# Attention heads kept stacked by partition, with their inverse row sums spread through DRAM, in an adaLN transformer block

## The chip, the cores and the metric

The kernel runs on one core of one Trainium2 chip. The metric is the device time of one execution in microseconds (us); less is better. The core's engines are TensorE (PE; its weight loads are PEld), VectorE (DVE), ScalarE (ACT), GpSimd (POOL) and SyncE (SP), which here issues nearly all DMAs, in program order, and waits in that order too.

## The reference

One transformer block on a sequence of 2048 rows with model width 448: layer norm with a modulation from a condition vector, windowed attention with 16 heads of width 28 (each row sees itself and the 255 rows before it), output projection, residual; then layer norm and modulation again and an MLP of width 1792 with the Mish function, and a residual.

```python
def _A_ref(x, wqkv, wo):          # H = 16, Dh = 28, W = 256
    q, k, v = qkv[0], qkv[1], qkv[2]
    scores = jnp.einsum("bhqd,bhkd->bhqk", q, k) * (Dh ** -0.5)
    mask = (idx[:, None] - idx[None, :] >= 0) & (idx[:, None] - idx[None, :] < W)
    p = _softmax(jnp.where(mask[None, None], scores, -1e9), axis=-1)
    o = jnp.einsum("bhqk,bhkd->bhqd", p, v)
    return o.transpose(0, 2, 1, 3).reshape(B, S, D) @ wo

h = _layernorm(x) * (1 + ca) + sa
x = x + ga * _A_ref(h, A_wqkv, A_wo)
h = _layernorm(x) * (1 + cb) + sb
x = x + gb * _B_ref(h, B_w1, B_b1, B_w2)     # dense, Mish, dense
```

## The kernel before

All large products are done in two halves: a number is split into a high part that the fast matmul type holds and a low remainder, and a product is high x high + high x low + low x high. So each operand has a "hi" copy (ScalarE) and a "lo" subtraction (VectorE or GpSimd).

The 2048 rows are four groups of 512. Group 0's norm and its first q and k tiles come first. q and k go to DRAM (`scr`) split and come back per head with `L`. Then runs the attention loop over u = 0 to 191, three steps per head, 48 steps per group. In each step TensorE does: the low and high half products with v of two older steps (`PV`, into a bank named pv), the scores of this step with their mask (`B`, bank sB), one or two score tiles whose row maxima VectorE takes (`A`, bank sA, two buffers), and some filler. ScalarE takes the exponential of sB twice (P and its high part Ph), GpSimd subtracts (`SP`: Pl = P - Ph), and Pl is multiplied two steps later. Every second head a transpose of the row maxima (`M2`, tile mt) and two small DMAs (q<-mr) put them back into q.

Filler is the other matmul work: q, k and v of the next group, the output projection of the group before, turns of the norm's output. Generators yield after each chunk with its estimated cost, and a credit of 0.56 to 0.87 per step (`RATE`) decides how many chunks a step takes. A filler that has nothing to do yields too and uses up the credit. Group 3 has no next group, so its filler ends near its step 28.

The part that is changed: after a head's last PV, `EV` (L751) copies 60 rows of pv (28 of V's high part, the row sums at row 28, from row 32 the 28 of V's low part) into one half of `o2`. For every pair of heads `E` (L759) turns that tile with four transposes into bank et, `E2` (L764, ScalarE) copies the low part, `E3` takes the reciprocal of the sums (L772, VectorE), adds the low part (L773, VectorE) and multiplies (L775, GpSimd) into `on`, where rows are sequence positions. When a group is full, `gen_oT` (TensorE L250, ScalarE L624, VectorE L619) turns it back, 16 transposes a group, into oh and ol, and `gen_wo` multiplies four 128-row tiles with wo, 11 matmuls each.

After the loop come nine more steps with the last PVs and the first MLP tiles (`TAIL`), then the MLP: for each group 14 f tiles, each 11 matmuls into z (`f1_mm`), Mish on ScalarE, and 12 into four acc banks (`ff2`). During the first group w1 and w2 are still being loaded and split (`pieces`, `piece_load`), group 3's projection runs as filler (`fill`), and the second group's norm as `fill2`. Ahead of this MLP loop SyncE issues `x1_load(0)`, pieces 4 to 8 of a list, and `x1_load(1)`.

Of the kernel before, what the change touches and what calls it, by code (L numbers as in the profile page):

```python
# [51 lines left out]
def adaln_block(ctx: ExitStack, tc: tile.TileContext, x, wqkv, wo, w1, b1, w2, c, w_mod, out):  # L52
# [36 lines left out]
    x1d = dram.tile([S, D], F32, name="x1d")  # L89
    xnd = dram.tile([NG - 1, GT, 512], F32, name="xnd")  # L90
# [221 lines left out]
    def tile_mms(p, ps):  # L312
        m = 0
        for n, (a, b) in enumerate(ps):
            PE.matmul(p, b, a, start=(n == 0), stop=(n == 10))  # L315
            m += 1
            if m >= chunk["v"] and n < 10:
                yield cost(m, p.shape[-1])
                m = 0
        return cost(m, p.shape[-1])  # L320
# [180 lines left out]
    first_tiles([(0, bank("pv", 1, "qk0_0")), (3, bank("tr", 1, "qk0_3"))])  # L501
# [17 lines left out]
    O2 = []  # L519
    for i in range(2):  # L520
        t = att.tile([128, GT], F32, name=f"o2_{i}")
        POOL.memset(t[32:64, :], 0.0)
        O2.append(t)
    wo3 = [mid.tile([128, D], F32R, name=f"wo3_{i}", tag="wo", bufs=7) for i in range(4)]
    wol = [mid.tile([128, D], F32R, name=f"wol_{i}", tag="wo", bufs=7) for i in range(3)]
# [25 lines left out]

    def gen_mod_wo():
# [7 lines left out]
        for ci in range(4):  # L560
            t = stg(qk, f"wop{ci}")
            pieces.append(t[:, 0:D])
            later.append(lambda ci=ci, t=t: load_piece(wo, ci, 0, D, t))
            yield
        yield
        flush()
        for ci in range(4):
# [5 lines left out]
            split_lo(w, wo3[ci], wol[min(ci, 2)], ci, DVE)  # L573
# [33 lines left out]
    on = {}  # L607
# [3 lines left out]
    on_full = set()  # L611
    XR = {g: {} for g in range(NG)}

    def gen_oT(g, tag, bufs, oT_pool, own=""):
        o = on[g]
        oh, ol = OT[g] = new_T(f"o{g}", oT_pool, own)

        def oT_out(p, ci):
            DVE.tensor_tensor(ol[:, ci], p, oh[:, ci].bitcast(F32), op=ALU.subtract)  # L619

        for ci in range(4):
            p = bank(tag, bufs, f"ot{g}{ci}")
            tr_chunk([o[:, t] for t in range(4)], ci, p)
            ACT.activation(oh[:, ci], p, AF.Copy)  # L624
            pipe.add(1, lambda p=p, ci=ci: oT_out(p, ci))
            if ci < 3:
                later.append(lambda t=ci: xr_load(g, t))
            yield
            if g == NG - 1:
                yield  # L630
# [6 lines left out]
    def gen_wo(g, tag, bufs, beside=None):  # L637
# [14 lines left out]
        for t in range(4):  # L652
# [12 lines left out]
            yield w  # L665
            if beside is not None and t:
                yield next(beside)
# [5 lines left out]
    mx, Pt, Ph, Pl, pvb, et, olt = {}, {}, {}, {}, {}, {}, {}  # L673
# [15 lines left out]
    def M2(pr):  # L689
        p = bank("tr", 1, f"mt{pr}")  # L690
# [56 lines left out]

    def EV(i):
        o = O2[i // 2 % 2][64 * (i % 2):64 * (i % 2) + 60]
        if i < NS - 3:  # L750
            ACT.activation(o, pvb[i][0:60, :], AF.Copy)  # L751
        else:
            DVE.tensor_copy(o, pvb[i][0:60, :])

    def E(pr):
        g, h = divmod(2 * pr, H)
        p = bank("tr", 1, f"et{pr}")
        for t in range(4):
            PE.transpose(p[:, t * 128:t * 128 + 124], O2[pr % 2][0:124, t * 128:(t + 1) * 128], ident[0:124, 0:124])  # L759
        et[pr] = p.rearrange("p (t a d) -> p t a d", t=4, a=2)  # L760

    def E2(pr):
        olt[pr] = att.tile([128, 4, 2, 28], F32, name=f"ol{pr}", tag="ol", bufs=1)
        ACT.activation(olt[pr], et[pr][:, :, :, 32:60], AF.Copy)  # L764

    def E3(pr):
        g, h = divmod(2 * pr, H)
        e, ol = et[pr], olt[pr]
        if h == 0:
            on[g] = mid.tile([128, 4, 512], F32, name=f"on{g}", tag="on")  # L770
        rc = att.tile([128, 4, 2, 1], F32, name=f"rc{pr}", tag="rc", bufs=2)
        DVE.reciprocal(rc, e[:, :, :, 28:29])  # L772
        DVE.tensor_tensor(ol, ol, e[:, :, :, 0:28], op=ALU.add)  # L773
        o = on[g][:, :, h * DH:(h + 2) * DH].rearrange("p t (a d) -> p t a d", a=2)
        POOL.tensor_tensor(o, ol, rc.to_broadcast([128, 4, 2, 28]), op=ALU.mult)  # L775
        if h == H - 2:
            POOL.tensor_copy(on[g][:, :, D:512], on[g][:, :, 384:448])
            on_full.add(g)
# [100 lines left out]
    def w2_split(f):  # L879
        n = NF - 1 - f  # L880
        pl = FW["p1"] if f == 0 else FW["ff"]
        w2h[f] = (mid.tile([128, D], F32R, name=f"w2h{f}", tag="wo", bufs=7) if n < 7 else
# [151 lines left out]
    credit = 0.0  # L1034
    for u in range(NU + 9):
# [21 lines left out]
        if s % 2 == 1 and 1 <= (s - 1) // 2 <= NS // 2:  # L1057
            pr = (s - 3) // 2
            if k == 2 and pr >= 0:
                E(pr)  # L1060
        if s % 2 == 0 and k < 2 and 0 <= (s - 4) // 2 < NS // 2:
            (E2, E3)[k]((s - 4) // 2)
# [81 lines left out]

# [62 lines left out]
```

## Time and profile before

| what | value |
|---|---|
| median of 3 runs | 705.66 us (704.79 to 706.11) |
| span of the profiled execution, first to last instruction | 703.9 us |
| the median less that span | 1.8 us |
| attention loop, first sB matmul to the start of its last step | 48.3 to 405.4 us |
| group starts in it (groups 1, 2, 3) | 122.0, 221.6, 321.8 us |
| MLP, first z matmul to the end | 406.7 to 703.9 us |
| granted TensorE clock | 1.000 |

The span runs from the first to the last instruction. The profiled execution is one execution; its time outside the span is not recorded, so it stands beside the runs by its span.

How to read it: a row of the groups gives line, engine, operation, output and inputs by tile names, shapes and count, then busy time, mean duration in ns, and the idle time before with what ended it. A row of the table of stretches gives the stretch in us from the span's start, its length and each engine's busy time with its number of instructions, then granted clock, DMA share and GB/s. A row of the chain of waits gives start, time on the chain, and what. A matmul's duration is longer than the time until the next one can start.

### The profile page before, as it was taken

The page shows a single profiled execution, that of the slowest core. Times are in us where ns is not written, and L with a number is a line of the kernel's source. Part 1 is how long each engine was busy: PE and PEld are TensorE (multiplying, and loading weights), DVE is VectorE, ACT ScalarE, POOL GpSimd, SP SyncE. Part 2 cuts the span into 40 slices and gives each one's busy share as a digit, 9 for nine tenths or more (in the row PEclk, how much of TensorE's full clock was granted, in tenths as well). Part 3 has the DMA queues.
Part 4 walks back from the last instruction along what each step waited for, and adds up shares of the span by engine and source line. Part 5 has one row for each costly group of instructions (what it writes and reads, how often), then busy time and mean ns, then how long its engine had stood idle before and what let it go on. Part 6 is the DMA issues. An engine that isn't in the chain of part 4 may idle for free.

```text
span 703.9 us, 11999 instructions
## 1 busy us (share of the span) xinstructions
PE 685.9 (97%) x4001; PEld 590.2 (84%) x4001; DVE 383.3 (54%) x1030; ACT 391.6 (56%) x740; POOL 326.4 (46%) x355
## 2 busy tenths in 40 slices
PE   9899999999999999999999899999999999999997
PEld 8777888888888888898887788878888888888886
DVE  5688658788655887655768755452224222421112
ACT  3628788777667867667878974344233323332221
POOL 6626779686666776666778957212010000000000
PEclk9999999999999999999999999999999999999999
DMA  7865664455662462663773165800350035001001
GB/s 209 259 221 188 208 204 152 139 181 157 181 209 76 158 207 88 185 211 95 226 216 120 54 203 170 227 20 1 104 117 4 0 106 119 1 1 52 1 1 52
DMA packets 75178, 90.16 MB, mean 128 GB/s; under 512 B 31535, under 2 KB 51741, under 8 KB 75117
## 3 DMA queue, kind: packets, MB, share of 16 engines
q1 hardware_dynamic: 74652, 89.39, 42.0%
q8 instruction: 32, 0.52, 0.3%
q14 instruction: 30, 0.24, 0.1%
q10 hardware_dynamic: 464, 0.00, 0.0%
HBM read 56.60 MB, written 32.51 MB: 127 GB/s over the span
## 4 chain that ended last, share of the span: by engine, by line
PE 78%; DVE 6%; DMA 6%; ACT 3%; POOL 3%; issue 3%; SPq 1%; DVEq 0%; POOLq 0%; ACTq 0%
PE z L917 17%; PE pv L745 10%; PE qk L315 8%; PE sA L683 5%; PE acc L1106 5%; PE acc L1104 5%; PE acc L1105 5%; PE sB L713 5%; PE wo L315 4%; PE qk_v L315 4%; PE sB L724 3%; DMA scr<-st 2%; PE et L759 2%; PE warm L428 1%; DVE junk L685 1%
## 5 line engine op out<-in xcount | busy, mean ns | idle before, releaser
L735 POOL TENSOR_TENSOR Pl<-P,Ph 128x512 fp32r<-128x512 f32 (+2 forms) x192 | 234.8, 1230 | 80.9 <-ACT Ph L728 46.6
L685 DVE CUSTOM_DVE_ANT_0 junk<-sA,mask 128x384 f32<-128x384 f32 (+2 forms) x256 | 135.1, 528 | 95.1 <-PE sA L683 87.4
L727 ACT ACTIVATE P<-sB 128x512 f32<-128x512 f32 (+2 forms) x192 | 109.6, 571 | 62.3 <-PE sB L724 58.1
L925 DVE TENSOR_TENSOR al<-t,ah 128x512 fp32r<-128x512 f32 x56 | 39.2, 700 | 181.8 <-ACT ah L924 181.8
L923 ACT ACTIVATE t<-z,b1c 128x512 f32<-128x512 f32 x56 | 38.3, 684 | 138.6 <-PE z L917 138.6
L728 ACT ACTIVATE Ph<-sB 128x512 fp32r<-128x512 f32 (+2 forms) x192 | 109.2, 569 | 0.0
L683 PE MATMUL sA<-k,q 84*128 84x384 f32 (+2 forms) x256 | 100.5, 396 | 1.8 <-DVE mx L685 1.1
L917 PE MATMUL z<-hlf,w 128*128 128x512 f32 x224 | 88.6, 395 | 0.0
L917 PE MATMUL z<-hhf,w 128*128 128x512 f32 x224 | 88.6, 395 | 0.0
L1104 PE MATMUL acc<-w2h,ah 128*128 128x448 f32 x224 | 82.2, 367 | 1.2 <-ACT ah L924 1.2
L1106 PE MATMUL acc<-w2h,al 128*128 128x448 f32 x224 | 82.1, 366 | 0.1
L1105 PE MATMUL acc<-w2l,ah 128*128 128x448 f32 x224 | 81.6, 364 | 0.0
L745 PE MATMUL pv<-Ph,v 128*60 128x256 f32 (+2 forms) x352 | 76.7, 292 | 0.6 <-ACT o L751 0.5
L745 PE MATMUL pv<-Pl,v 128*60 128x256 f32 (+2 forms) x352 | 74.0, 284 | 2.4 <-POOL Pl L735 1.4
L713 PE MATMUL sB<-q,k 86*128 86x256 f32 (+1 forms) x352 | 74.2, 285 | 0.5 <-DMA q<-mr 0.5
L917 PE MATMUL z<-hhf,w1l 128*128 128x512 f32 x168 | 66.3, 395 | 0.0
L713 PEld LDWEIGHTS sB<-q,k 86*128 86x128 f32 x352 | 61.5, 189 | 2.3 <-DMA q<-mr 1.5
L724 PE MATMUL sB<-fdmask,identr 128*128 128x128 bf16 (+1 forms) x320 | 60.1, 253 | 0.0
L745 PEld LDWEIGHTS pv<-Ph,v 128*60 128x60 f32 x352 | 45.8, 133 | 14.0 <-ACT o L751 1.9
L745 PEld LDWEIGHTS pv<-Pl,v 128*60 128x60 f32 x352 | 45.2, 132 | 11.5 <-POOL Pl L735 3.8
L683 PEld LDWEIGHTS sA<-k,q 84*128 84x128 f32 x256 | 48.9, 193 | 7.0 <-DVE mx L685 4.3
L917 PEld LDWEIGHTS z<-hlf,w 128*128 128x128 f32 x224 | 42.2, 188 | 10.0
(159 smaller groups left out, 1252.4 us busy)
## 6 DMA issues: line engine op xcount, KB each, us to landing
scr<-st SPq DMA_DIRECT2D x24, 512.0 KB
k<-scr SPq DMA_DIRECT2D x48, 252.0 KB
q<-scr SPq DMA_DIRECT2D x64, 168.0 KB
scr<-st SPq DMA_DIRECT2D x32, 256.0 KB
x<-x1d SPq DMA_DIRECT2D x10, 448.0 KB
xin<-in_A_x_dram SPq DMA_DIRECT2D x8, 448.0 KB
xr<-in_A_x_dram SPq DMA_DIRECT2D x16, 224.0 KB
x1d<-xr SPq DMA_DIRECT2D x16, 224.0 KB
```

Source lines behind the costliest of these rows:

```text
L315: PE.matmul(p, b, a, start=(n == 0), stop=(n == 10))
L683: PE.matmul(p[:, c0:384], q[0:84, t * 128:(t + 1) * 128], k[0:84, t * 128 + c0:t * 128 + 384], start=True, stop=True)
L685: DVE.tensor_tensor_reduce(out=junk[:, c0:384], in0=p[:, c0:384], in1=mask[:, c0:384], scale=1.0, scalar=-3.0e38, op0=ALU.add, op1=ALU.max ...
L713: PE.matmul(p[:, c:c + 128 * (t1 - t0)], k[:, jj * 128:(jj + 1) * 128], q[:, t0 * 128:t1 * 128], start=(n == 0), stop=False, skip_group_ch ...
L727: ACT.activation(P[:, c0:], p[:, c0:], AF.Exp, scale=SCALE)
L728: ACT.activation(Ph[u][:, c0:], p[:, c0:], AF.Exp, scale=SCALE)
L735: eng.tensor_tensor(Pl[u][:, a:b], Pt[u][:, a:b], Ph[u][:, a:b].bitcast(F32), op=ALU.subtract)
L745: PE.matmul(pv[0:60, t0 * 128:t1 * 128], V[j % NV][:, h, :], P[u][:, c:c + 128 * (t1 - t0)], start=(P is Ph and b == 0 and n == 0), stop=F ...
L917: PE.matmul(zb[n], ps[m][1], ps[m][0], start=(m == 0), stop=(m == 10))
L1104: PE.matmul(p, ah[n][:, ts], w2h[f], start=(f == 0), stop=False)
L1105: PE.matmul(p, ah[n][:, ts], w2l[f], start=False, stop=False)
L1106: PE.matmul(p, al[n][:, ts], w2h[f], start=False, stop=(f == NF - 1))
```

## The change

Head outputs are no longer turned. `EV` puts each head into 32 partitions of `on[:, ci]` (four heads a tile, 16 heads in four tiles): ScalarE copies rows 0 to 31 of pv, and VectorE adds the low part's 28 rows in place. The row sums then stand in one partition per head. For each quad of heads, four DMAs spread the sums over 32 partitions of 16 numbers (`sums`), VectorE takes 128x16 reciprocals (`inverse`), one DMA stores them to DRAM (`spread`, tensor rcd), four DMAs read each head's 512 numbers back into 32 partitions (`gather`, tile r4), and GpSimd multiplies the whole tile (`divide`). Counted from step 14 + 12n of the loop, these come at steps 4, 5, 7 and 9 for quad n; `sums` comes one step after each `EV`. Then `split_o` makes hi and lo from `on` at once, without transposes. The tile's 32 rows a head hold 28 numbers, so wo is loaded to 32 rows a head with zeros between, and each wo tile has 12 matmuls, not 11. The last quad's gather is issued after the loop and its divide stands in `gen_split`, in the MLP's first steps. mt moves to the sA banks and pv has two banks.

```diff
-    first_tiles([(0, bank("pv", 1, "qk0_0")), (3, bank("tr", 1, "qk0_3"))])
+    first_tiles([(0, bank("pv", 2, "qk0_0")), (3, bank("pv", 2, "qk0_3"))])
...
+    def wo_rows(ci, t):
+        for j in range(4):
+            r = (4 * ci + j) * DH
+            dma(t[32 * j:32 * j + DH], wo[r:r + DH, :])
...
-            t = stg(qk, f"wop{ci}")
-            pieces.append(t[:, 0:D])
-            later.append(lambda ci=ci, t=t: load_piece(wo, ci, 0, D, t))
+            t = stg(qk, f"wop{ci}")[:, 0:D]
+            pieces.append(t)
+            POOL.memset(t, 0.0)
+            later.append(lambda ci=ci, t=t: wo_rows(ci, t))
...
-    def gen_oT(g, tag, bufs, oT_pool, own=""):
...
+    def split_o(g, ci, pl, own):
+        if ci == 0:
+            OT[g] = new_T(f"o{g}", pl, own)
+        oh, ol = OT[g]
+        ACT.activation(oh[:, ci], on[:, ci], AF.Copy)
+
+        def low():
+            DVE.tensor_tensor(ol[:, ci], on[:, ci], oh[:, ci].bitcast(F32), op=ALU.subtract)
+            if ci == 3:
+                on_split.add(g)
...
+        pipe.add(1, low)
+
+    def split_ready():
+        if ready and (ready[0][0] == 0 or ready[0][0] - 1 in wo_done) and ready[0][0] < NG - 1:
+            split_o(*ready.pop(0), att, "o")
+
+    def gen_split(g):
         for ci in range(4):
...
+            if ci == 3:
+                divide(4 * g + 3)
                 yield
+            split_o(g, ci, FW["ff"], "")
+            yield
...
-            for ci in range(3):
+            for ci in range(4):
                 ps += [(oh[:, ci, ts], wo3[ci]), (oh[:, ci, ts], wol[ci]), (ol[:, ci, ts], wo3[ci])]
-            ps += [(oh[:, 3, ts], wo3[3]), (ol[:, 3, ts], wo3[3])]
...
-        p = bank("tr", 1, f"mt{pr}")
+        p = bank("sA", 2, f"mt{pr}")
...
-            pvb[i] = bank("sA", 2, f"pv{i}") if NS - 3 <= i < NS - 1 else bank("pv", 1, f"pv{i}")
+            pvb[i] = bank("pv", 2, f"pv{i}")
...
     def EV(i):
-        o = O2[i // 2 % 2][64 * (i % 2):64 * (i % 2) + 60]
+        g, h = divmod(i, H)
+        ci, j = divmod(h, 4)
+        o, rows = on[:, ci], slice(32 * j, 32 * j + 32)
         if i < NS - 3:
-            ACT.activation(o, pvb[i][0:60, :], AF.Copy)
+            ACT.activation(o[rows], pvb[i][0:32, :], AF.Copy)
         else:
-            DVE.tensor_copy(o, pvb[i][0:60, :])
-
-    def E(pr):
...
-    def E3(pr):
...
+            DVE.tensor_copy(o[rows], pvb[i][0:32, :])
+        a = o[32 * j:32 * j + DH]
+        DVE.tensor_tensor(a, a, pvb[i][32:60, :], op=ALU.add)
+
+    def sums(i):
...
+        dma(sm[i // 4][32 * j:32 * j + 32], on[32 * j + DH:32 * j + DH + 1, ci].rearrange("o (r n) -> o r n", n=16))
+
+    def inverse(n):
+        DVE.reciprocal(sm[n], sm[n])
+
+    def spread(n):
+        dma(rcd[n], sm[n])
+
+    def gather(n):
+        rows = rcd[n].rearrange("(j r) n -> j (r n)", j=4)
+        for j in range(4):
+            dma(r4[32 * j:32 * j + 32], rows[j:j + 1].to_broadcast([32, 512]))
+
+    def divide(n):
+        g, ci = divmod(n, 4)
+        POOL.tensor_tensor(on[:, ci], on[:, ci], r4, op=ALU.mult)
+        ready.append((g, ci))
...
-            while g - 1 not in on_full:
+            while g - 1 not in on_split:
                 yield
-            yield from gen_oT(g - 1, "mm", 2, att, "o")
...
+    def quads(u):
+        split_ready()
+        if (u - 3) % 3 == 0 and 0 <= (u - 6) // 3 < NS:
+            sums((u - 6) // 3)
+        n, v = divmod(u - 14, 12)
+        for n, v in ((n, v), (n - 1, v + 12)):
+            if 0 <= n < NQD and v in QSTEP:
+                QSTEP[v](n)
+
+    QSTEP = {4: inverse, 5: spread, 7: gather, 9: divide}
...
+    gather(NQD - 1)
     x1_load(0, ff)
...
-    fill = chain(gen_oT(NG - 1, "tr", 2, ff), gen_wo(NG - 1, "tr", 2), finish())
+    fill = chain(gen_split(NG - 1), gen_wo(NG - 1, "tr", 2), finish())
```

TensorE in group 2, step 7: before, between this step's two sA tiles and the next step's sB.

```order
L683 MATMUL sA_1_3581<-k_1_144,q_0_377 128x384
L250 MATMUL ot_3591<-ident,on_2299 128x128 x4
L683 MATMUL sA_2_3599<-k_1_144,q_0_377 128x384
L745 MATMUL pv_3531<-Ph_3515,v_166 60x128
L745 MATMUL pv_3531<-Ph_3515,v_174 60x384
L745 MATMUL pv_3531<-Pl_3545,v_166 60x128
L745 MATMUL pv_3531<-Pl_3545,v_174 60x384
L713 MATMUL sB_3609<-q_2_460,k_4_150 128x384
```

And the same place now.

```order
L696 MATMUL sA_1_3538<-k_1_145,q_0_378 128x384
L696 MATMUL sA_2_3542<-k_1_145,q_0_378 128x384
L758 MATMUL pv_3487<-Ph_3476,v_167 60x128
L758 MATMUL pv_3487<-Ph_3476,v_175 60x384
L758 MATMUL pv_3487<-Pl_3501,v_167 60x128
L758 MATMUL pv_3487<-Pl_3501,v_175 60x384
L726 MATMUL sB_3552<-q_2_461,k_4_151 128x384
```

The four ot transposes are gone, and nothing stands in their place: steps 7 to 12 of groups 1 and 2 hold no filler, and the first wo matmul stands in step 13, where it was step 11.

VectorE in steps 7 to 9 of group 2: before (junk and mx are the row maxima, hlo the low half of the turned output, st that of a q or k tile, mr the row maxima on their way back into q).

```order
L339 TENSOR_TENSOR st_6_3557<-qk_6_3466,st_6_3557 128x512
L619 TENSOR_TENSOR hlo_3590<-ot_3591,hho_3589 128x512
L685 ISA junk,mx_3451<-sA_3_3620,mask 128x384
L685 ISA mx_3451 128x1
L619 TENSOR_TENSOR hlo_3590<-ot_3623,hho_3589 128x512
L685 ISA junk,mx_3646<-sA_0_3647,mask 128x384
L685 ISA mx_3646 128x1
L693 CAST mr_3652<-mt_3650 8x128
```

And now, at the same place.

```order
L340 TENSOR_TENSOR st_6_3514<-qk_6_3426,st_6_3514 128x512
L772 TENSOR_TENSOR on<-on,pv_3487 28x512
L698 ISA junk,mx_3410<-sA_3_3563,mask 128x384
L698 ISA mx_3410 128x1
L698 ISA junk,mx_3582<-sA_0_3583,mask 128x384
L698 ISA mx_3582 128x1
L706 CAST mr_3588<-mt_3586 8x128
```

The two low halves have left this place (the group's four stand where each quad is ready, the last in step 13), and the add of a head's low part to `on` has come in ahead of the reductions, as it does for every head.

SyncE at the end of the attention loop: before, from the last pieces of the loop to `x1_load(1)`.

```order
L59 DMA w2p_6138<-in_B_w_dram 128x448
L59 DMA x_0_6232<-x1d 128x2x448 x2
L59 DMA w1p_6235<-in_B_w_dram 128x448
L59 DMA w1p_6237<-in_B_w_dram 64x448 x2
L59 DMA w2p_6240<-in_B_w_dram 128x448
L59 DMA w1p_6242<-in_B_w_dram 128x448
L59 DMA w1p_6244<-in_B_w_dram 128x448
L59 DMA x_1_6246<-x1d 128x2x448 x2
```

And now (sm are the row sums of a quad and then their inverses, rcd the tensor in DRAM, r_479 the tile r4).

```order
L59 DMA w2p_5975<-in_B_w_dram 128x448
L59 DMA sm_5911<-on 32x1x16 x2
L59 DMA rcd<-sm_5911 128x16
L59 DMA r_479<-rcd 32x512 x4
L59 DMA x_0_6094<-x1d 128x2x448 x2
L59 DMA w1p_6097<-in_B_w_dram 128x448
L59 DMA w1p_6099<-in_B_w_dram 64x448 x2
L59 DMA w2p_6102<-in_B_w_dram 128x448
L59 DMA w1p_6104<-in_B_w_dram 128x448
L59 DMA w1p_6106<-in_B_w_dram 128x448
L59 DMA x_1_6108<-x1d 128x2x448 x2
```

The last quad's chain, sums to DRAM and back, now stands ahead of x1 and of the pieces of w1 and w2 on the queue that issues them all.

More of the change, by code (lines that the diff above doesn't have):

```diff
@@ L517, in adaln_block @@
     k3_tile(att, NK - 1)
[L519 to L525, printed above, removed]
+    wo3 = [mid.tile([128, D], F32R, name=f"wo3_{i}", tag="wo", bufs=8) for i in range(4)]
+    wol = [mid.tile([128, D], F32R, name=f"wol_{i}", tag="wo", bufs=8) for i in range(4)]
     def xr_tile(name):
@@ L755, in E @@
-    def E(pr):
[L756 to L764, printed above, removed]
-    def E3(pr):
[L767 to L778, printed above, removed]
+            DVE.tensor_copy(o[rows], pvb[i][0:32, :])
@@ L1056, in adaln_block @@
             load_slot(s + LEAD + 2)
[L1057 to L1062, printed above, removed]
+        quads(u)
         if g < NG:
```

39 lines of the change are left out of this document (20 added, 19 removed).

## The prediction

> **What bounds the kernel now.** I read the page's head, then the stretches of the span, the groups of instructions, the chain of waits and at last the timeline of SyncE. The page comes first.
>
> ```profile
> span 703.9 us, 11999 instructions
> PE 685.9 (97%) x4001; PEld 590.2 (84%) x4001; DVE 383.3 (54%) x1030; ACT 391.6 (56%) x740; POOL 326.4 (46%) x355
> ```
>
> TensorE is busy for 97% of the span, so time that leaves TensorE can leave the span, where no other engine is full too. The table of stretches shows where that is. The first row is steps 7 to 12 of group 1 (counted by the sB matmuls on TensorE's timeline) and the second the same of group 2, which repeats group 1 almost to the instruction; then come steps 13 to 19 and 20 to 27 of group 1, and last steps 28 to 39 of group 3. After the length come the busy times of PE, PEld, DVE, ACT and POOL.
>
> ```profile
> 137.62:149.38 11.76, 11.24 (x86) 9.64 (x84) 10.53 (x30) 10.14 (x21) 10.29 (x12) 1.00 0.63 195
> 237.50:249.26 11.76, 11.26 (x85) 9.64 (x84) 10.54 (x30) 10.16 (x22) 10.26 (x12) 1.00 0.65 198
> 149.38:163.30 13.92, 13.92 (x99) 12.53 (x98) 11.44 (x35) 9.72 (x19) 9.95 (x11) 1.00 0.68 220
> 163.30:179.83 16.53, 15.78 (x114) 13.85 (x114) 13.77 (x40) 12.60 (x24) 11.26 (x10) 1.00 0.30 93
> 376.22:395.61 19.39, 17.18 (x128) 13.97 (x127) 16.58 (x48) 16.60 (x33) 18.86 (x20) 1.00 0.19 58
> ```
>
> In all but the last TensorE leads, but VectorE is at 82 to 90%, and GpSimd at 87% in the first: a second bound is close. In the last row GpSimd is the bound (18.86 of 19.39), because group 3 has no filler work left; what leaves TensorE there saves nothing.
>
> **The change part by part.** *Transposes out, wo passes in.* These rows are from the chain of waits (start, time on the chain) and from the timeline (start, duration).
>
> ```profile
> 111.73 0.43 PE et L759 x4
> 146.38 0.82 PE wo L315 x4
> 415.77 1.03 PE L250 MATMUL ot<-ident,on 128*128 128x128 f32 x8
> 416.56 0.48 PE L917 MATMUL z<-hhf,w 128*128 128x512 f32 x1
> L759 PE MATMUL et<-ident,o 124*128 124x124 f32 x128 | 18.8, 269 | 0.0
> ```
>
> Four et transposes hold the chain 0.43 us; eight ot transposes start at 415.77 and the next matmul at 416.56, 0.395 for four. A mean of 269 ns is one transpose's latency, and they overlap. So 32 x 0.43 + 16 x 0.395 = 20.1 us leave. A wo pass takes 0.82/4 = 0.205, and 16 more come in: 3.3. By place: group 0 loses 7 et groups, 3.0 us. Groups 1 and 2 lose 8 et and 4 ot groups and gain 4 passes, 3.44 + 1.58 - 0.82 = 4.2 each. Group 3 as long as it has filler loses 4 et and 4 ot groups, 1.72 + 1.58 - 0.82 = 2.5. Together 13.9; the rest lies in the last steps of group 3 or at the turn to the MLP, and comes below.
>
> The Trainium skill, TensorE: Matmul & The Clock Gate, Part 4 (PE-mode transpose), gives about 275 ns for a transpose inside a kernel; 192 of them would be an estimated 52.8 us instead of 20.1. The trace agrees on the one (269) and not on a row of them (0.43 for four).
>
> *The wait for the last quad.* In steps 7 to 12 of groups 1 and 2 the filler now yields with nothing: the ot transposes are gone, and wo starts in step 13, since the last quad is divided in step 11 and its low half made in step 13 (before, wo started in step 11). TensorE keeps 11.24 - 1.58 - 0.43 - 8 x 0.205 = 7.6 us there. GpSimd's 10.29 loses one head-pair product and the 64-column copy and gets one divide.
>
> ```profile
> L735 POOL TENSOR_TENSOR Pl<-P,Ph 128x512 fp32r<-128x512 f32 (+2 forms) x192 | 234.8, 1230 | 80.9 <-ACT Ph L728 46.6
> L775 POOL TENSOR_TENSOR on<-ol,rc 128x224 f32<-128x224 f32 x32 | 18.3, 573 | 21.7 <-DVE ol L773 9.1 <-ACT Ph L728 8.9 <-PE ot L250 1.5
> L777 POOL COPY on<-on 128x256 f32<-128x256 f32 x4 | 1.6, 396 | 0.3
> L619 DVE TENSOR_TENSOR hlo<-ot,hho 128x512 fp32r<-128x512 f32 x16 | 10.9, 685 | 5.7 <-ACT hho L624 5.7
> L772 DVE RECIPROCAL rc<-et 128x8 f32<-128x8 f32 x32 | 6.5, 202 | 1.1 <-ACT ol L764 1.1
> L773 DVE TENSOR_TENSOR ol<-ol,et 128x224 f32<-128x224 f32 x32 | 10.7, 335 | 0.0
> L751 ACT ACTIVATE o<-pv 60x512 f32<-60x512 f32 x61 | 35.9, 589 | 22.7 <-PE pv L745 22.3
> ```
>
> A divide is a 128x512 product of two fp32 tiles, like Pl: 1.24. That makes 10.29 - 0.57 - 0.40 + 1.24 = 10.6, of which one instruction can be left over to the next steps: 9.3 at the least. So the six steps shrink to some 9.4, not by the 3.65 taken out of TensorE but by 2.3, and 1.64 of wo comes back later. Cost 1.4 in each of groups 1 and 2, 0.8 in group 3, where the wait is shorter (wo from step 15 to step 13): 3.6. If GpSimd's lag were free it would be nothing.
>
> *More work for VectorE.* Each of 64 heads gets an add of 28x512 out of PSUM, 0.685 by the nearest row (L619, PSUM and SBUF in), and each pair loses 0.202 + 0.335; the 16 low halves stay. It is queued behind ScalarE's copy of the same head (0.589), and behind it stand the row-maximum reductions that free the two sA banks. In steps 13 to 27 VectorE has 11.44 + 13.77 = 25.2 us; plus 5 x 0.685 and one reciprocal of 0.2, less 2.5 x 0.54: 27.5, in 30.45 less 2.5 x 0.43 = 29.4, or 94%, before any wait for ScalarE. Nothing if the waits fall into gaps, up to 3.5 if all five copies' 0.589 are waited out there; I take 1.0 in groups 1 and 2, 0.5 in group 0, 0.3 in group 3: 2.8. In the last 20 steps, where no gain is to be had, two adds stand among the VectorE splits of the last heads: 0.5.
>
> ```profile
> PE pv L745 <- ACT o L751: 0.5, 2, 0.3
> PE sA L683 <- DVE mx L685: 1.1, 3, 0.4
> 90.00:100.00 10.00, 10.00 (x67) 8.00 (x65) 5.64 (x22) 7.56 (x18) 6.57 (x8) 1.00 0.78 241
> L522 POOL MEMSET o<- 32x512 f32 x2 | 1.0, 518 | 0.1
> ```
>
> The small edits I cost at nothing: pv in two banks (TensorE waits 0.5 in all for ScalarE's o), mt in an sA bank (sA waits 1.1 in all for VectorE), 16 wo loads for 5, and four clears on GpSimd in group 0, where it has a third of its time free. Without that cover the clears would be 4 x 0.52 = 2 us.
>
> Attention so far: -13.9 + 3.6 + 2.8 + 0.5 = -7.0.
>
> *The turn to the MLP.* The last quad's inverse sums go SBUF, DRAM, SBUF on SyncE's queue ahead of x1 and the w1 and w2 pieces. Before, these loads waited for nothing but memory that the last PV frees:
>
> ```profile
> 409.96 0.40 PE L745 MATMUL pv<-Pl,v 128*60 128x128 f32 x2
> 412.03 0.69 DVE L753 COPY o<-pv 60x512 f32<-60x512 f32 x1
> 408.64 1.54 SPq L59 DMA_DIRECT2D x<-x1d  x2
> 410.24 1.74 SPq L59 DMA_DIRECT2D w1p<-in_B_w_dram  x3
> 413.12 3.80 DMA w1p<-in_B_w_dram
> 45.64 2.49 DMA q<-mr
> 318.54 3.15 DMA q<-mr
> 40.05 1.69 DMA q<-scr
> 446.59 4.37 SPq L59 DMA_DIRECT2D z<-xnd  x8
> 415.54 0.34 SPq L59 DMA_DIRECT2D w2p<-in_B_w_dram  x1
> 416.47 1.03 ACT L192 ACTIVATE w<-w1p 128x448 fp32r<-128x448 f32 x2
> 417.92 1.15 POOL L198 TENSOR_TENSOR w1l<-w1p,w 128x448 fp32r<-128x448 f32 x1
> 419.15 1.42 POOL L200 TENSOR_TENSOR w<-w1p,w 64x448 fp32r<-64x448 f32 x1
> 421.98 0.48 PE L917 MATMUL z<-hhf,w 128*128 128x512 f32 x1
> 424.98 0.45 PE L1104 MATMUL acc<-w2h,ah 128*128 128x448 f32 x1
> ```
>
> On before's clock: the last head's copy ends at 412.7. Its sums are issued in 0.35 and fly 2.5 as q<-mr does: 415.6. Reciprocal, 0.2: 415.8. Store, 0.35 + 2.5: 418.65, and the first gather waits on SyncE for that landing. Four gathers at 4.37/8 = 0.55: 420.85. Two x loads, 1.54: 422.4, where w1p was issued at 410.24, so the hold is 12 us. With 0.58 an issue and 3 us of flight piece 6 lands at 426.0 and piece 7 (two loads) at 427.1; z of the fourth f tile needs them (421.98 before). ScalarE takes the two (0.52 each) ahead of three copies of on (0.6, as o), so the second of these and its low half are there at 429.5, the six wo passes ahead of that z end at 430, z at 432.5. The second six passes need the last quad's divide, which stands on GpSimd behind piece 7 (429.8 with 1.15 and 1.42) and a w2 and two w1 splits of 1.15, the first waiting for ScalarE: 434.2; divide 435.4, ScalarE 436.0, low half 436.7. So acc of the third f tile starts at 436.7 and not at 424.98, with 36 wo passes left instead of 44 (8 x 0.205 = 1.6): a loss of 11.7 - 1.6 = 10.1, in which the last et and ot groups are contained. With flights of 1.7 (q<-scr's) and 0.35 an issue it is 7.5; with 3.15 and loads of 3.8, 12.
>
> The Trainium skill, DMA: Bandwidth & Descriptors, Anatomy of one DMA, puts about 2.0 us of fixed cost on each DMA, most of it the receipt of the write, heaviest to HBM, and lets the issuing sequencer do the waiting: that rule speaks against two dependent round trips. By it two flights would be 1.0 shorter, the loss an estimated 9.1; q<-mr took 2.49 and 3.15 here.
>
> **The sum.** 703.9 - 7.0 + 10.1 = 707.0. The median of the runs, 705.66 (704.79 to 706.11), lies 1.8 above the profiled span; with that, 708.8, so 709.
>
> **The rivals.** *Forecast*, chance 0.58: 704 to 714, from attention gains of 3 to 10 and a loss at the turn of 7.5 to 12. A measurement can tell about 0.2% (1.4 us) from no change; of this case 0.41 is slower, 0.15 within it, 0.02 faster.
>
> *The hold is covered*, 0.24. If pieces 6 and 7 land before about 420 on before's clock (the sums of the last head leaving early, the gathers in a burst), the turn costs at most 3 and attention keeps 8 to 10: 696 to 703, say 700. For it: ScalarE took these pieces only after other work. Against it: the order of SyncE's queue and flights of 2.5. 0.22 is faster, 0.02 within.
>
> *Waits inside the steps*, 0.16. GpSimd's divide stands two steps behind its gather, 2 x 1.96 = 3.9 us, and the gather needs 4 x 0.55 + 2.5 = 4.7. Waiting 0.8 for 15 quads is 12 us on GpSimd, with a split per step queued behind; half of it past GpSimd's slack gives 6: 715, up to 720. It decides once the landing comes after GpSimd reaches the divide. Against it: GpSimd reaches a step late. All of it is slower.
>
> *Every transpose costs its latency*, 0.02: 192 x 0.269 = 51.6 instead of 20.1, so 677. The 0.43 for four speaks against it; this is what the skill's page on TensorE would give.
>
> Sums: slower 0.57, within 0.17, faster 0.26. From 700 to 715 about 0.1 is left out on each side.
>
> **What would show it.** Right: no et and ot rows, 64 wo rows of each of three kinds; in steps 7 to 12 of groups 1 and 2 TensorE idle behind Pl or sA; group 0 about 3 us shorter; SyncE silent for some 10 us after the last PV, then x and w1p; ScalarE waiting for w1p, TensorE idle ahead of the fourth f tile and of wo. Wrong: w1p issued within 4 us of the last PV, or issued late with TensorE dense after it; Pl late behind the divide in every quad, or the reciprocal waiting for sums, would mean the third case.

## The result, and the profile after

The changed kernel takes 764.18 us (median of 4 runs, 760.89 to 767.91) against 705.51 us before (704.79 to 706.11): ratio 1.0828, 95% interval 1.0788 to 1.0868. 709 was predicted, 700 to 715. The profiled execution took 762.61 us, its span is 760.8. The page of the profile after, its head and the granted clock:

```profile
span 760.8 us, 11973 instructions
PE 691.9 (91%) x3825; PEld 583.7 (77%) x3825; DVE 425.2 (56%) x1046; ACT 387.9 (51%) x708; POOL 331.2 (44%) x337
...
PEclk9999897999999989999999998899999999999999
```

TensorE executes 176 matmuls fewer (192 transposes out, 16 wo passes in) and is yet busy for 6.0 us more; and it is not busy for 760.8 - 691.9 = 68.9 us, before for 18.0. The clock explains most of the first. By the prediction's own terms 20.1 - 3.3 = 16.8 us of work left, so 669.1 was to be expected, and 22.8 us are too much. The mean granted clock was 0.97 (before 1.000): in eight stretches, 44.4 us together, it was 0.50. TensorE was busy for 36.0 us of these, work that takes 18.0 at full clock, so the clock accounts for some 18 of the 22.8; the rest is not explained. So the loss of 56.9 in the span is 50.9 more of idle time and 22.8 of slower work, less 16.8 of work.

By place: the first z matmul starts at 451.62, before at 406.71, so attention lost 44.9 where a gain of 7.0 was predicted; from there to the end it is 309.2 against 297.2, a loss of 12.0 where 10.1 was predicted. Group 0 of the attention loop, predicted to be some 3 us shorter, is 16.2 longer (48.1 to 138.0, before 48.3 to 122.0), groups 1 and 2 are 9.7 and 7.0 longer.

What TensorE and GpSimd wait for in the kernel after (us in total, times, longest):

```profile
PEld pv L758 <- POOL Pl L748: 28.0, 17, 4.4
PE pv L758 <- POOL Pl L748: 23.3, 12, 4.1
PEld sA L696 <- DVE mx L698: 14.2, 28, 1.6
PE wo L316 <- ACT hho L621: 7.0, 2, 5.9
PE sB L726 <- DMA q<-mr: 4.8, 2, 2.5
...
POOL on L796 <- DMA r<-rcd: 12.7, 3, 6.9
POOL on L796 <- ACT Ph L741: 10.7, 3, 4.7
POOL on L796 <- PE pv L758: 6.4, 2, 3.2
POOL on L796 <- DMA k<-scr: 5.7, 1, 5.7
POOL on L796 <- PE qk L316: 4.9, 1, 4.9
POOL on L796 <- ACT on L768: 2.9, 2, 1.4
POOL on L796 <- DMA q<-scr: 2.8, 1, 2.8
POOL on L796 <- PE sA L696: 2.4, 1, 2.4
POOL on L796 <- DVE Pl L748: 0.6, 1, 0.6
```

(The rows are put together by engine; waits of other engines stand between them.) Before, by the PE rows, sA waited 1.1 for VectorE and pv 1.4 for Pl. `on L796` is the divide. Of what is named as its releaser only the gather (r<-rcd) and the head's copy and add feed it. A wait is put down to the event that came last by the profile, so Ph, pv, qk and k stand here for the gather: each of these divides starts 1.7 to 3.0 us after the last gather of its quad was issued. That is 49.1 us in fifteen waits, 3.3 us each, so every quad in the steps waits.

One of them, on the timelines of SyncE, GpSimd and TensorE (start, duration):

```profile
83.44 1.47 SPq L59 DMA_DIRECT2D q<-mr  x2
85.01 0.58 SPq L59 DMA_DIRECT2D sm<-on  x1
85.68 1.93 SPq L59 DMA_DIRECT2D r<-rcd  x4
```

```profile
90.63 1.26 POOL L796 TENSOR_TENSOR on<-on,r 128x512 f32<-128x512 f32 x1 [5.67 <-DMA k<-scr]
91.85 3.37 POOL L748 TENSOR_TENSOR Pl<-P,Ph 128x512 fp32r<-128x512 f32 x3
```

```profile
88.66 0.40 PE L758 MATMUL pv<-Ph,v 128*60 128x128 f32 x2
93.17 0.68 PE L758 MATMUL pv<-Pl,v 128*60 128x128 f32 x2 [4.10 <-POOL Pl L748]
```

SyncE can't issue the gathers before 85.68, because it stands ahead of q<-mr until VectorE has the row maxima (83.44) and then issues these and the next head's sums first. The gathers land at 90.6 by the start of the divide; three Pl are queued behind it, and TensorE stands still from 89.06 to 93.17. The same stretch by single microseconds (after the busy times the granted clock, DMA share, GB/s):

```profile
90.00:91.00 1.00, 0.00 (x0) 0.00 (x0) 0.00 (x0) 0.00 (x0) 0.37 (x1) 0.97 0.87 334
91.00:92.00 1.00, 0.00 (x0) 0.00 (x0) 0.00 (x0) 0.08 (x1) 1.00 (x2) 0.50 1.01 385
...
93.00:94.00 1.00, 0.83 (x4) 0.81 (x4) 1.00 (x3) 0.21 (x2) 1.00 (x2) 0.50 0.56 181
...
97.00:98.00 1.00, 1.00 (x7) 0.95 (x7) 0.33 (x3) 0.48 (x2) 0.20 (x1) 0.62 0.57 137
98.00:99.00 1.00, 1.00 (x8) 0.83 (x7) 0.97 (x3) 0.53 (x3) 0.53 (x1) 1.00 0.00 0
```

From 90.9 to 97.8 the clock is half: TensorE works on from 93.17 at half speed for 4.6 us more.

The turn to the MLP, SyncE's timeline after:

```profile
457.66 0.51 SPq L59 DMA_DIRECT2D sm<-on  x1
460.87 0.34 SPq L59 DMA_DIRECT2D rcd<-sm  x1
462.34 1.72 SPq L59 DMA_DIRECT2D r<-rcd  x4
464.15 0.90 SPq L59 DMA_DIRECT2D x<-x1d  x2
465.09 1.67 SPq L59 DMA_DIRECT2D w1p<-in_B_w_dram  x3
```

This is the prediction's order and hold: silent between the steps of the chain, 6.9 us from the last sums to w1p, and TensorE then stands 5.87 us ahead of wo.

### The profile page after: what moved, and what is told of

It reads as the page before. It is cut to its first block, busy times and chain, and to the rows that moved or that the text cites. A ratio compares the mean times of both kernels' runs of the same rounds, so it can differ in the third digit from the quotient of the medians.

```text
span 760.8 us, 11973 instructions
## 1 busy us (share of the span) xinstructions
PE 691.9 (91%) x3825; PEld 583.7 (77%) x3825; DVE 425.2 (56%) x1046; ACT 387.9 (51%) x708; POOL 331.2 (44%) x337
## 4 chain that ended last, share of the span: by engine, by line
PE 64%; DVE 11%; DMA 8%; issue 5%; ACT 5%; SPq 4%; POOL 3%; POOLq 0%; DVEq 0%; ACTq 0%
PE z L936 16%; PE pv L758 8%; PE qk L316 5%; PE acc L1132 5%; PE acc L1131 5%; PE acc L1130 5%; PE wo L316 4%; PE sA L696 4%; SPq L59 4%; PE sB L726 4%; DVE junk L698 3%; PE qk_v L316 3%; PE sB L737 2%; DMA scr<-st 2%; POOL Pl L748 2%
## 5 line engine op out<-in xcount | busy, mean ns | idle before, releaser
L696 PE MATMUL sA<-k,q 84*128 84x384 f32 (+2 forms) x256 | 102.8, 407 | 11.3 <-DVE mx L698 7.0
L758 PE MATMUL pv<-Pl,v 128*60 128x256 f32 (+2 forms) x352 | 76.9, 293 | 23.5 <-POOL Pl L748 23.3
L726 PE MATMUL sB<-q,k 86*128 86x256 f32 (+1 forms) x352 | 76.9, 293 | 5.8 <-DMA q<-mr 4.8
L726 PEld LDWEIGHTS sB<-q,k 86*128 86x128 f32 x352 | 64.3, 197 | 8.1 <-issue 5.4
L737 PE MATMUL sB<-fdmask,identr 128*128 128x128 bf16 (+1 forms) x320 | 62.0, 260 | 0.0
L772 DVE TENSOR_TENSOR on<-on,pv 28x512 f32<-28x512 f32 x64 | 43.6, 681 | 15.0 <-ACT on L768 13.8
```

The costliest lines, as they stand in the source:

```text
L696: PE.matmul(p[:, c0:384], q[0:84, t * 128:(t + 1) * 128], k[0:84, t * 128 + c0:t * 128 + 384], start=True, stop=True)
L726: PE.matmul(p[:, c:c + 128 * (t1 - t0)], k[:, jj * 128:(jj + 1) * 128], q[:, t0 * 128:t1 * 128], start=(n == 0), stop=False, skip_group_ch ...
L758: PE.matmul(pv[0:60, t0 * 128:t1 * 128], V[j % NV][:, h, :], P[u][:, c:c + 128 * (t1 - t0)], start=(P is Ph and b == 0 and n == 0), stop=F ...
```

## The experiments

Theories. A: the divide's wait for the gather holds GpSimd, and Pl behind it. B: the 64 adds hold VectorE. C: the quad's nine DMAs crowd SyncE and the transfers, so that q, k and the row maxima come late. D: mt in an sA bank holds the score tiles. The expectations split C in two: C1 is SyncE's issues and waits, C2 the transfers themselves. "Attention" is the start of the first z matmul in the one profiled execution, "MLP" the rest of its span; e5 and e6, whose medians agree, differ by 7.9 in attention, so less than about 8 is not read from that column.

| kernel | median us | ratio to before (95%) | attention | MLP |
|---|---|---|---|---|
| before | 705.51 | | 406.7 | 297.2 |
| after | 764.18 | 1.0828 (1.0788 to 1.0868) | 451.6 | 309.2 |
| e1 divide five steps later | 761.40 | 1.0790 (1.0750 to 1.0830) | 451.8 | 309.9 |
| e2 divide by a constant, no chain | 731.69 | 1.0385 (1.0353 to 1.0417) | 424.8 | 303.8 |
| e3 chain moved, nobody waits | 755.47 | 1.0716 (1.0677 to 1.0756) | 441.9 | 308.6 |
| e4 no adds | 750.73 | 1.0648 (1.0617 to 1.0680) | 440.2 | 308.6 |
| e5 neither chain nor adds | 713.20 | 1.0099 (1.0069 to 1.0130) | 407.9 | 303.4 |
| e6 as e5, mt own bank | 712.95 | 1.0099 (1.0070 to 1.0129) | 415.8 | 301.0 |
| e7 before, mt in sA | 705.90 | 1.0004 (0.9994 to 1.0014) | 406.1 | 297.2 |
| e8 last chain behind the loads | 758.72 | 1.0761 (1.0722 to 1.0801) | 451.6 | 305.8 |
| e9 3 DMAs a quad | 787.33 | 1.1158 (1.1115 to 1.1202) | 468.6 | 312.9 |
| e10 adds a step later | 768.37 | 1.0899 (1.0840 to 1.0958) | 455.4 | 308.2 |
| e11 before plus 9 DMAs a quad | 725.60 | 1.0302 (1.0258 to 1.0347) | 422.6 | 300.5 |
| e12 four mends | 758.60 | 1.0752 (1.0712 to 1.0792) | 447.5 | 305.7 |
| e13 3 DMAs, steps moved apart | 755.08 | 1.0712 (1.0686 to 1.0738) | 445.0 | 307.0 |
| e14 before plus 3 DMAs a quad | 713.43 | 1.0114 (1.0088 to 1.0139) | 415.4 | 296.5 |
| e15 before, twelve late splits | 776.84 | 1.1020 (1.1004 to 1.1037) | 479.7 | 297.2 |
| e16 as e5, divide 8 steps earlier | 713.21 | 1.0110 (1.0071 to 1.0150) | 408.3 | 303.9 |
| e17 as e13, chain on ScalarE's queue | 759.22 | 1.0762 (1.0741 to 1.0784) | 453.5 | 304.7 |
| e18 as e6, transposes put back | 718.04 | 1.0184 (1.0147 to 1.0221) | 416.0 | 301.4 |

**e1, e2, e3: the wait, or the DMAs.**

```diff
-    QSTEP = {4: inverse, 5: spread, 7: gather, 9: divide}
+    QSTEP = {4: inverse, 5: spread, 7: gather, 14: divide}      (e1)
+    QSTEP = {9: divide}, r4 set to ones, no sums(), no gather    (e2)
-        POOL.tensor_tensor(on[:, ci], on[:, ci], r4, op=ALU.mult)
+        POOL.tensor_tensor(on[:, ci], on[:, ci], on[:, ci], op=ALU.mult)    (e3)
```

> Theory A (the divide waits on GpSimd for the gathered inverses; the splits behind it come late, TensorE runs dry and then gets half its clock for some us): with the divide five steps later (14 instead of 9, some 10 us after its gather) GpSimd's 18 us of waiting for the gather go, most of TensorE's idle gaps behind Pl go, and of attention's 45 us some 30 to 40 come back: 722 to 735, granted clock back to 0.99. Theory B (the 64 adds on VectorE hold the row maxima and the low halves): no change, within 3 us. Theory C (SyncE's queue, crowded by nine small DMAs a quad and 16 loads of wo, brings q, k and the row maxima late): no change, within 5 us. The turn to the MLP costs its 12 in each.

> Leaves out the division: no row sums, inverses, store or gathers are moved; GpSimd multiplies by a tile of ones at the same step. Theories A and C: both the waits in the steps and the hold at the turn go, so that the time falls by 45 to 65: 698 to 720 (698 if the predicted gain of 7 in attention is real behind the waits). Theory B: the adds are still there, so only the turn's 12 come back: 750.

> Leaves out the division in another way: sums, inverses, store and gathers are all issued as before, but GpSimd multiplies the outputs by themselves, so that nothing waits for the gather. Theory A: as with the later divide or a little lower, 715 to 735, since only the wait is gone. Theory C: hardly any change, 755 to 765, since SyncE's queue is as full as it was. Theory B: no change.

Theory A alone falls: in e1 no divide waits any more, and its interval can't be told from that of after. With the divide out of the way, the next waits stand in the same places; those of e1:

```profile
PEld sA L696 <- DVE mx L698: 21.3, 34, 2.0
...
PE sA L696 <- DVE mx L698: 11.8, 21, 1.5
...
PE sB L726 <- DMA q<-mr: 8.4, 6, 3.4
...
PE sA L696 <- DMA k<-scr: 7.0, 5, 2.5
```

e2, without chain, is 32.5 us faster than after, 26.8 of them in attention. e3, where the DMAs fly and nobody waits, gets 8.7 of these. So of attention's 26.8 the wait is worth 9.7 at the most (nothing by e1) and the DMAs by themselves, with the sixteen reciprocals that e3 keeps, 17.1. That is theory C, and the 26 us that e2 still lacks to before are something else.

**e4, e5: the adds.** e4 drops the two lines of `EV` that add `pvb[i][32:60]`; e5 is e2 and e4 together.

> Leaves out the add of the low part of v to each head's outputs (64 instructions of 0.68 us on VectorE). Theory A: the adds hide, 0 to 6 us less: 758 to 764. Theory B: 30 us or more less: 715 to 735. Theory C: 0 to 3 less.

> Leaves out the division (as in e2) and the add of the low part of v (as in e4). The four runs so far: without the division's DMAs 32.5 us less, without the adds 13.5 less. Theory C with B in second place (SyncE's crowded queue and VectorE's adds, each on its own): they add up, 764.2 - 32.5 - 13.5 = 718. If the adds only cost because the DMAs make VectorE's inputs late (theory C alone): 728 to 732. If nothing but the two is wrong with the change, the predicted 14 us of saved transposes come out: 692 to 698.

Theory B holds beside C: the adds cost 13.5 us with the chain there, a size that none of the expectations had, and 18.5 without it (731.69 - 713.20). What TensorE waits for VectorE shows it; first e2, then e5:

```profile
PEld sA L696 <- DVE mx L698: 18.3, 34, 1.6
PEld mt L704 <- DVE mx L698: 9.9, 14, 1.6
PE sA L696 <- DVE mx L698: 9.9, 19, 1.4
```

```profile
PEld sA L696 <- DVE mx L698: 9.8, 16, 1.7
...
PE sA L696 <- DVE mx L698: 5.6, 11, 1.5
...
PEld mt L704 <- DVE mx L698: 2.9, 6, 0.7
```

**e10: is it the adds' wait for ScalarE, or their time?**

```diff
+        if u > 3 and (u - 4) % 3 == 2 and (u - 4) // 3 < NS:
+            AD((u - 4) // 3)            # the add, out of EV, ahead of the next step's PV
```

(The move of the sums goes a step later too.)

> After, with each head's add of the low part of v (and the move of its row sums) one step later, so that it stands at the head of VectorE's step, long after ScalarE's copy. If the adds cost by making VectorE wait for ScalarE (13.8 us in 26 waits) ahead of the row maxima: 8 to 13 us less, 751 to 756. If they cost by VectorE's 43.6 us of work: within 3 us of after.

No gain, which points to the 43.6 us of VectorE's time that the adds take. It doesn't settle it: VectorE's reciprocal then waited for the later sums (9.5 us in six waits), which may have eaten up what the move saved.

**e6, e7: the banks.**

```diff
-        p = bank("tr", 1, f"mt{pr}")
+        p = bank("sA", 2, f"mt{pr}")       (e7, in the kernel before; e6 is the reverse, in e5, with pv in one bank)
```

> As e5, and the transposed row maxima (mt) get a PSUM bank of their own again, with one bank for pv, as before the change. Theory D (mt in the sA pair: TensorE cannot start a score tile before VectorE is through with the maxima of two tiles and both copies of mt): sA no longer waits for VectorE, some 32 times 0.5 us, 12 to 18 less than e5: about 700 to 705, and nearer 692 if the steps are then free of waits. Rival (the bank costs nothing, as predicted): the same as e5 within 3 us.

> The kernel before with one edit, mt in an sA bank. Theory D: 10 to 18 us slower than before, 715 to 723, with TensorE's sA and mt waiting for VectorE's mx. Rival (as predicted, nothing): 705 to 707.

Theory D falls in both; the prediction's "nothing" for the banks holds there. With the chain and the adds in place it was not tried.

**e11, e14: the DMAs alone.** `sums`, `spread` and `gather` of the change are put into the kernel before, in the same steps, with nobody who reads what they bring; the gathers go to DRAM there, not to SBUF. e14 has one DMA for each.

> The kernel before, which computes all that it did, and in addition moves a row of each head's outputs, stores four of them and gathers them in four DMAs, in the same steps as after, into memory that nobody reads (the gather's target is in DRAM, for want of space). Theory C: SyncE's queue alone makes it 10 to 20 us slower, 716 to 726, with sB waiting for q<-mr. Rival (SyncE had room, and the DMAs cost only where someone waits for them): within 3 us of before.

> As e11 (the kernel before with added DMAs that nobody waits for), with the same bytes in 3 DMAs a quad instead of 9. Theory C1: a third of the issues and so about a third of e11's loss of 20, 710 to 714. Theory C2: the loss stays, 722 to 727.

Theory C shown by itself: nine DMAs a quad cost a kernel that doesn't need them 20 us, three cost 8, as C1 had it. More than half of e11's loss in attention, 9.1 us, lies in group 0, where SyncE also loads weights. TensorE waits in e11 for k and for the maxima on their way into q, which it did for 0.4 and 0.5 us in before:

```profile
PE sA L684 <- DMA k<-scr: 10.5, 9, 2.8
...
PE sB L714 <- DMA q<-mr: 3.7, 3, 1.6
```

SyncE's issuing in group 1, summed over its timeline, was 41 us of 99.6 before and 67 of 109.3 after: the DMAs that the change adds take SyncE 0.4 to 0.6 us each by the median, as much as the large ones, and the queue stands at each until its data are there.

**e9, e13, e17, e12: fewer DMAs in the changed kernel.**

```diff
+        dma(sm[i // 4], on[DH:128:32, ci].rearrange("j (r n) -> j r n", n=16))
...
+        dma(r4, rcd[n].rearrange("(j o r) n -> j o (r n)", j=4, o=1).to_broadcast([4, 32, 512]))
...
+    QSTEP = {6: inverse, 7: spread, 10: gather, 15: divide}     (e13, e17)
```

(In e13 and e17 the last quad's chain also goes behind the loads, about as in e8.)

> After, with the same bytes in 3 DMAs a quad instead of 9: one moves the row sums of four heads, one stores the inverses, one gathers them over all partitions (the 16 loads of wo stay). Theory C1 (SyncE's issue time and its waits: 68 us of a group's 109 are issuing, against 43 of 100 before): 6 fewer issues of some 0.55 us a quad give q, k and the row maxima back their lead, 12 to 20 us less than after, 744 to 752. Theory C2 (the transfers themselves, or the chain of three flights, are what costs): within 4 us of after.

> After with 3 DMAs a quad, the steps of the chain moved apart (inverse two steps later, store two, gather three, divide six) so that no engine reaches a step of it before its input has landed, and the last quad's chain behind the loads. Theory C1 (issues and waits on SyncE's queue): near the run without any of these DMAs, 730 to 738. Theory C2 (the transfers themselves): 750 to 760.

> As e13, with the three DMAs of a quad issued from ScalarE's queue and not from SyncE's (the last quad's store and gather stay on SyncE's). If their place in SyncE's queue is what costs: 12 to 20 less than e13, 735 to 743, little of it lost again on ScalarE (3 issues of 0.5 us a quad, 24 us in all, in an engine that is busy half the time). If the transfers cost, by lengthening the flights of q and the maxima: within 5 of 755, or slower by what the issues take from ScalarE.

> After with four mends: 3 DMAs a quad (e9), the divide three steps later, the store and the gather of the last quad behind the loads of x1, w1 and w2 (e8), the adds one step later (e10). If the costs are SyncE's queue, the divide's wait, the hold and the adds' wait, each on its own: 764 - 15 - 5 - 5.5 - 10 = about 728; e5, with neither division nor adds, took 713 and should be a floor. If they only hide one another: 740 to 750.

e9 and e12 do nothing of what was expected, and e9 is 23 us slower than after; e13 and e17 come out where C2 had put them. The three DMAs are not the nine in another packing: the four gathers of 64 KB land 1.7 to 3.0 us after the last is issued; the one of 256 KB lands after 4.3 to 7.7 in the waits of e9 and e13, and q<-mr takes 2.1 to 6.2 in the seven waits of e13, 1.3 and 3.7 in the two of after. From e13, SyncE, then GpSimd, then TensorE:

```profile
115.90 0.59 SPq L59 DMA_DIRECT2D r<-rcd  x1
117.00 1.39 SPq L59 DMA_DIRECT2D q<-mr  x2
```

```profile
124.17 1.27 POOL L795 TENSOR_TENSOR on<-on,r 128x512 f32<-128x512 f32 x1 [3.75 <-DMA r<-rcd]
```

```profile
124.61 0.41 PE L726 MATMUL sB<-q,k 86*128 86x384 f32 x1 [4.16 <-DMA q<-mr]
```

The gather's issue ends at 116.49 and it lands at 124.17, 7.7 us later, and q<-mr (118.39) at 124.61. The Trainium skill, DMA: Bandwidth & Descriptors, Why a DMA increments its semaphore by 16 and not by 1, says that a DMA runs on the largest number of engines, up to 16, that divides the outermost dimension of both its patterns. This gather's outermost dimension is 4, and 32 in each of the four; by that rule it would run on 4 engines and each of the four on 16. The flights agree with it; a gather of 256 KB in another shape was not run, so this stays argued. e17 speaks against SyncE's queue as what holds these three: from ScalarE's queue the kernel is no faster, though their issues then take ScalarE's time. e12 made a wait of its own, VectorE's reciprocal for the later sums (14.7 us in twelve waits).

**e8: the turn.** The store and the gathers of the last quad go behind `x1_load(1, p1)`.

> After, with the store and the gathers of the last quad's inverse sums issued behind the loads of x1, w1 and w2. If the turn's loss is the hold of SyncE's queue (the prediction's term of 10.1): 8 to 12 us less than after, 752 to 756, and TensorE's idle 5.9 us ahead of wo gone. If the last quad's divide or the wo passes bound the turn anyhow: 0 to 4 less, 760 to 764.

5.5 us less by the medians, which misses both ranges of the expectation and is hardly clear of the spread of after (the intervals touch); 3.4 of it shows in the MLP. SyncE issues w1p at 459.30 instead of 465.09, and the wait of 5.87 ahead of wo is gone; but the store is then issued at 464.65 and the gathers only at 470.41, and wo waits three times, 4.5 us in all, for the last splits.

**e15: what a wait costs.**

```diff
-        for eng, a, b in ((POOL, c0, 512),) if u < NU - 5 else ((POOL, 0, 256), (DVE, 256, 512)):
+        for eng, a, b in ((POOL, c0, 512),) * (6 if u % 14 == 6 and u < 174 else 1) if u < NU - 5 else ((POOL, 0, 256), (DVE, 256, 512)):
```

> The kernel before, with the split of one block in fourteen done six times over on GpSimd (the same result, 5 x 1.23 = 6.2 us of delay, twelve places). TensorE then waits for Pl in each by what GpSimd's lead of about two steps does not cover, 2 to 4 us: 24 to 48 us in all, if waits are all. If each wait also costs the half clock that after shows behind its gaps (some 3.4 us at 0.5, so 1.7 a gap): 20 more, and the mean granted clock falls to about 0.97.

Twelve idle gaps ahead of pv stand in TensorE's timeline, 2.5 to 6.2 us long, 50.4 us together. The span is 73.0 longer. The head of the page:

```profile
span 776.9 us, 12059 instructions
PE 709.6 (91%) x4001; PEld 607.2 (78%) x4001; DVE 382.9 (49%) x1030; ACT 393.2 (51%) x740; POOL 397.6 (51%) x415
```

The same 4001 matmuls are busy for 23.7 us more than before: on average each gap costs 2.0 us on top of its 4.2, and the mean granted clock is 0.96.

**e16, e18: why e5 stays above before.** e16: `QSTEP = {1: divide}` in e5. e18: in e6,

```diff
+            p = bank("tr", 1, f"et{s}")
+            for t in range(4):
+                PE.transpose(p[:, t * 128:(t + 1) * 128], ident, ident)
```

> As e5 (neither division nor adds; the multiplication by ones stays), with the multiplication eight steps earlier, straight behind the last head's copy. If the wait for the last quad in steps 7 to 12 of groups 1 to 3 (the prediction's 3.6, by now with half-clock stretches behind the gaps) is what keeps e5 above the predicted gain: 5 to 12 less than e5, 701 to 708. If TensorE is held by other waits in those steps: within 3 of 713.

> As e6 (neither division nor adds, mt with a bank of its own), and in addition 32 times four 128x128 transposes into that bank where et stood, of data that nobody reads. The prediction's term (0.43 us of TensorE for each four, all of it on the path): 713 + 13.8 = 727. If TensorE no longer sets the pace of the steps, so that the time of the transposes was not to be had: 711 to 717, or less, if they keep the granted clock up.

e16 changes nothing: the wait for the last quad is not what holds the steps. e18: 128 transposes cost 5.1 us by the medians, not 13.8. The heads of their pages, e6 and then e18:

```profile
span 716.8 us, 11580 instructions
PE 681.9 (95%) x3825; PEld 580.2 (81%) x3825; DVE 384.4 (54%) x966; ACT 387.1 (54%) x708; POOL 331.4 (46%) x338
```

```profile
span 717.4 us, 11836 instructions
PE 687.6 (96%) x3953; PEld 588.4 (82%) x3953; DVE 386.1 (54%) x966; ACT 387.4 (54%) x708; POOL 332.8 (46%) x338
```

In these two executions TensorE is busy for 5.7 us more and idle for 5.1 less (34.9 and 29.8), at a mean clock of 0.993 against 0.983, as if the transposes filled time in which TensorE would wait. But e6's is the slowest of its ten (718.59, median 712.95), and e18's is not, so the two are no fair pair; the 5.1 of the medians is what stands.

## Why the prediction was wrong

The sign was right by luck, and the size is off by 55: the forecast had "slower" from a turn that outweighs a gain, and most of the loss, 44.9 of 56.9, is in attention, where -7.0 was predicted. By difference of the profiled executions, after to e2 to e5 to before, the chain in the steps is 26.8 of it, the adds 16.9, and the rest of the change 1.2, each to some 8 us.

- **The step that failed first: the chain of DMAs has no term in the sum for attention.** The turn's chain was worked out queue position by queue position; the same chain stands in the steps fifteen times, and there only the third rival spoke of it, and only of the divide. Nine DMAs a quad, moved in past q<-mr, q and k on SyncE, were priced at nothing. They cost 20 us where nobody waits for them (e11) and 17.1 of attention here (e3 to e2), where q, k and the row maxima come later (sB waits 8.3 us for q<-mr in e3, 1.8 in e2).
- **"Waits inside the steps"** (0.16) named the right wait. Its size was 12 us on GpSimd, and 49.1 were measured: it took the gather as issued in its step, but in the wait shown SyncE stood ahead of q<-mr first. And the wait's price is not the loss: e1 takes it away, and TensorE waits more for the maxima and the loads instead (sA for VectorE 11.8 where it was 7.0, q<-mr 8.4 for 4.8, k 7.0 for 2.0).
- **"More work for VectorE", 2.8**, was mis-sized: by the medians the adds cost 18.5 without the chain and 13.5 with it. The working was a share, 94% in steps 13 to 27, with a bound of 3.5 from ScalarE's copies (five of 0.589 are 2.9). An engine at 94% that stands in the loop from scores to maxima to scores has little slack to hide 0.68 us a head in; that this work, and not the wait for ScalarE's copy, is what counts is likely by e10 and not shown.
- **"Transposes out", -20.1**: the work left TensorE, the time didn't follow. With chain and adds gone, attention is at 407.9 where the prediction's own terms (-13.9, 3.6) give 396.4, and putting the et transposes back costs 5.1 of 13.8 (e18). In before TensorE was busy 97%; that other waits stood just beneath it is what these two say, but no run names them.
- **"The wait for the last quad", 3.6**: not found (e16).
- **No step knew of the clock.** Idle time was priced at its own length. In after some 18 us come on top for work at half clock (e15: 2.0 for each gap of 4.2).
- **"The turn to the MLP", 10.1**: 12.0 measured, the order as told, but that the sum came so near is partly luck. The hold is only part of it: without any chain (e2) the MLP still is 6.6 longer than before, so the chain is worth 5.4, and loads ahead of it bring 3.4 (e8). Of the 6.6, 5.2 are idle time of TensorE: in e2's MLP it waits 2.6 us ahead of wo for the last splits, 1.4 for an output tile and 1.0 for a split of w2, and in before's for none of these. Why these come late there is not settled. The estimate of 9.1 beside the sum takes its 2.0 us a flight from a section of the Trainium skill (DMA: Bandwidth & Descriptors, Anatomy of one DMA — SWDGE (gpsimd) path) on DMAs that GpSimd issues; SyncE issues these, and the gathers' flights were 1.7 to 3.0 (after).
- **The small edits at nothing**: right for the banks (e7). The 16 loads of wo were not tried alone; e5 and e6 have them, and their group 0, where they are issued, takes 73.3 and 77.1 us against 73.7, so at the most they are worth a few us there.

The second rival (the hold is covered) and the fourth (every transpose costs its latency) are out: w1p was issued 6.9 us after the last sums, and 128 transposes cost 5.1 us in e18, not 128 x 0.269.

What stays open: how the 17.1 of the DMAs divide between SyncE's issues and the transfers. e14 against e11 says that number counts. e13 and e17 say that the transfers count, but only for the one gather of 256 KB, which is slow by itself; they leave the nine undecided. No kernel here that does the whole work beats before.

## What to carry to other kernels

When a change puts DMAs into a loop, price each of them as an issue on its queue, with what the queue waits for and what stands behind it, also where nobody is in a hurry for the data. When work leaves an engine that is busy 97%, look for the waits just beneath it before booking the gain. And book an idle gap of TensorE at more than its length: here, for gaps of 4.2 us on average, at about one and a half times.

## What the runs showed of the hardware

- TensorE's granted clock can fall to 0.50 behind an idle gap and stay there for some us. In e15 a gap of 2.51 us (118.58) was followed by half clock from 122.3 to 125.7, and one of 2.61 (147.96) by none. In e5 two gaps of 1.08 and 1.50 within 7 us were enough, while one of 2.05 (277.40) was followed by none:

```profile
145.00:146.00 1.00, 0.62 (x5) 0.61 (x6) 0.00 (x0) 0.00 (x0) 1.00 (x2) 0.89 0.83 185
146.00:147.00 1.00, 1.00 (x6) 0.90 (x6) 0.50 (x3) 0.76 (x2) 1.00 (x2) 0.50 0.89 310
...
148.00:149.00 1.00, 1.00 (x4) 0.91 (x4) 1.00 (x1) 0.92 (x2) 0.98 (x1) 0.50 1.14 299
149.00:150.00 1.00, 1.00 (x8) 0.86 (x7) 1.00 (x3) 0.17 (x1) 0.70 (x1) 0.90 0.78 133
```

  The Trainium skill, TensorE: Matmul & The Clock Gate, Part 1, tells of a free-running window of some 3.4 us, half clock after an idle one and full clock after a busy one. The half and the length (3.4 us in both cases) agree; its advice to avoid gaps above about 3.4 us is too mild here, since gaps of 1 to 2.5 us can do it too.
- A small DMA takes SyncE as long to issue as a large one: median 0.57 us for 2 KB of sums, 0.41 for a gather of 64 KB, 0.69 for the 4 KB of q<-mr.
- One broadcast gather of 256 KB took 4.3 to 7.7 us from the end of its issue to land (e9, e13), the last of four with 64 KB each 1.7 to 3.0 (after).
